# Alternating PSUM bank sets, pairing logit sums, and splitting the last outputs over two engines in a fused attention and gMLP kernel

## The chip, the core and the metric

The kernel runs on one core of a Trainium2 chip. The time is the device time of one execution in microseconds (us). A run gives several timed executions, and one execution is profiled. The span of a profiled execution is 1.7 to 1.8 us shorter than its device time in the runs here. An execution counts as slow when it is over 1.5% above the fastest of the same kernel, and as fast otherwise; all times compared here are of fast executions unless the text says otherwise.

Names of engines in the profile: PE is TensorE (matmuls), PEld its weight loads, DVE is VectorE, ACT is ScalarE, POOL is GpSimd, SP is SyncE, which here only issues DMAs. PSUM (`ps` in the profile) is the memory into which PE writes its sums; the kernel uses it in banks. "SPq", "ACTq" are the queues of DMA issues on those engines.

## The reference

One input `x` of 2048 tokens by 512 features goes through a layer norm, and then through two branches whose sum is added to `x`.

```python
# A: sliding, dilated local attention; 32 heads of 16, window of 8 keys, 2 apart
q, k, v = split(xn @ wqkv)                       # wqkv 512 x 1536
logits  = einsum('bhsd,bhswd->bhsw', q, kg) * scale   # kg: a token's own key and 7 earlier ones
o       = einsum('bhsw,bhswd->bhsd', softmax(logits), vg)
A       = o @ wo
# B: gMLP; w_sp mixes all 2048 tokens
z       = gelu(xn @ w_in)                        # w_in 512 x 1792
z1, z2  = z[..., :896], layernorm(z[..., 896:])
g       = w_sp @ z2 + b_sp                       # w_sp 2048 x 2048
B       = (z1 * g) @ w_out
return x + A + B
```

## The kernel before

The kernel describes its work as tasks with the data that they read and write. A scheduler in the kernel's own Python simulates the engines from estimated durations and fixes **one order of tasks for each engine** before the program is built.

Work goes by blocks of 512 tokens (`tc` or `j`, 0 to 3). The product `w_sp @ z2` has seven columns of features. Block 0 takes all seven with plain products. Blocks 1 to 3 take three pairs of columns by seven smaller products each (a Winograd-like scheme), and the last column with plain products. A product sequence uses PSUM banks 0 and 1 and a set of two more, banks 2 and 3 or banks 4 and 5:

```python
def prod7(i, tc, gap):
    sl = n_cb[0] % 2
    n_cb[0] += 1
    X, Wb, V, Y = 0, 1, 1, 2 + 2 * sl          # Y, Z: the alternating set
    Z = Y + 1
    ...
    P(1, X, ...)                               # 8 matmuls into bank X
    gap()                                      # other matmuls are put in here
    P(5, Wb, ...)                              # needs Tn1, a weight sum made by VectorE
    cp(half(Y), half(X), ...)                  # ScalarE copies X to Y ...
    P(6, Y, ...)                               # ... before P6 adds to it
    P(2, X, ...); gap()
    P(7, Z, ...)                               # needs wB1 after VectorE's in-place sum
    P(3, Y, ...); gap()
    P(4, V, ...)                               # needs Tn4
    # VectorE: the merge (reads Y and Z), then the product with z1 ("u")
    T("dve", ... tensor_tensor(cb, PC(512 * Y, ...), wtt, ALU.add), reads=[("ps", Y), ("ps", Z), ...], name="mg")
    T("dve", ... tensor_tensor(z1T, cb, z1T, ALU.mult), name="u")
```

The plain products advance the same counter, because they share the copy buffer `cb`:

```python
def plain_slices(tc, bank_of, cuts=(4, 4, 4, 4), fc=FC - 1):
    ...                                        # 16 matmuls into one bank
    sl = n_cb[0] % 2
    n_cb[0] += 1
    cv = A("cb", 512, 1024 * sl)
    cp(cv, bank(k), ...)                       # ScalarE empties the bank
    T("dve", ... tensor_tensor(uv, cv, uv, ALU.mult), name="up")
```

The logits: VectorE multiplies queries and shifted keys for a quarter `c` of the features (a "logit product", 128 x 4096), and PE sums over the features with weights of 128 x 32, four column tiles of the array side by side:

```python
def prod_reduce(j, c):
    T("dve", ... tensor_tensor(pbv, qb, kb, ALU.mult), writes=[("pb", s_)], prio=FILL)
    def mm(t):
        for wh in range(2):
            for g in range(4):                 # four column tiles
                last = t.matmul(PC(32 * g * PR + 3072 + 512 * wh, [[1, 512]], 32), E8[c], pb[s_],
                                start=(c == 0), stop=(c == 3))
        return last
    T("pe", mm, reads=[("pb", s_), "E8"], writes=["psl"], margin=800.0)
```

The output of a 128-token tile is summed in one bank, copied out by ScalarE and stored from ScalarE's queue (`cp(A("yout", ...), po, ...)`, then `dma("act", ...)`).

Two more pieces are used by experiments: a small bias difference that VectorE makes for each of the blocks 1 to 3, and the loads of V for the attention:

```python
def bdiff(tc):
    T("dve", ... tensor_tensor(bdt[:, 0:256], bbc_right, bbc_left, ALU.subtract), reads=["bbc"], writes=["bd"])
def ld_V(j, par):                              # even and odd tokens of block j, 1.15 MB each
    return dma("sp", lambda e: e.dma_start(A("Ve", 4608, 4608 * par), src), ...)
```

## Time and profile before

The time before is 242.76 us (median of 3, 242.71 to 243.29). The profiled execution has a span of 242.4 us; its own device time was 244.2 us.

| what | value | where it is read |
|---|---|---|
| PE busy | 235.1 us, 97% of the span | busy time by engine |
| VectorE busy | 195.4 us, 81%; 31.4 of 32 us between 172 and 204 us | windows |
| PE waits after the start | 2.5 us, two waits | list of waits |
| one group of logit sums | 0.55 us, and 0.11 us more for the run after it | chain of waits |
| end without matmuls | 3.4 us | timeline |

The page of the kernel before: span and busy tenths in 40 equal slices.

```profile
span 242.4 us, 3719 instructions
...
PE   7999999999999999999999999999699999999994
...
DVE  3687879989989998999989999769999999912010
```

PE is full from the second slice to the last but one, except in slice 29, where the longer of the waits below lies. VectorE is busy for seven tenths or more in every slice from the third to the thirty-fifth, but for one with six. The windows view of the kernel before has, for each stretch, its length and then busy us and instruction counts of PE, PEld, DVE, ACT and POOL, the granted clock, the DMA share and GB/s:

```profile
25.00:94.00 69.00, 69.00 (x413) 28.34 (x412) 63.79 (x83) 54.95 (x112) 30.39 (x31) 1.00 0.57 136
...
133.00:172.00 39.00, 37.76 (x266) 26.33 (x264) 34.93 (x29) 16.59 (x38) 0.00 (x0) 1.00 0.95 229
172.00:204.00 32.00, 30.82 (x225) 22.32 (x225) 31.38 (x27) 15.18 (x36) 0.00 (x0) 1.00 0.57 153
```

Between 25 and 94 us PE has no gap at all. Between 133 and 204 us it loses 2.4 us. PE's list of waits in the kernel before (total us, times, longest) names the cause:

```profile
PE ps L1089 <- ACT ps L1016: 2.5, 2, 2.0
```

L1089 is the matmul of the seven products, L1016 is every copy by ScalarE. The timeline of the kernel before around the longer of the two waits (start, duration, instruction; in brackets the idle time of that engine just before it, and who ended it):

```profile
159.53 2.29 DVE L1138 TENSOR_TENSOR arena<-arena 128x4096 bf16<-128x4096 bf16 x1 [3.20 <-DMA arena<-vscr]
...
171.67 0.68 DVE L1113 TENSOR_TENSOR arena<-ps,wtt 128x512 bf16<-128x512 f32 x1
172.38 0.37 ACT L1016 ACTIVATE ps<-ps 128x256 f32<-128x256 f32 x1 [3.64 <-DVE arena L1113]
...
172.81 1.92 PE L1089 MATMUL ps<-arena 128*128 128x256 bf16 x16 [2.04 <-ACT ps L1016]
```

Read upwards: PE stood 2.04 us, because ScalarE's copy into the bank stood for VectorE's merge L1113, which reads that bank. This is the border between block 1 and block 2, where two product sequences in a row use banks 2 and 3.

The chain of waits of the kernel before (start, us, what) around one group of logit sums L764:

```profile
81.81 4.32 PE ps L870 x20
86.12 0.55 PE ps L764 x8
86.67 0.97 PE ps L870 x4
```

A 512-column matmul takes 0.216 us in a long run (20 of them 4.32 us). A group of 8 is two waves of four, ideally 0.43 us; it takes 0.55, and the four matmuls after it 0.97 instead of 0.86. So a group costs 0.12 us at its start and 0.11 us at its end.

The tail of the kernel before, timeline:

```profile
239.29 0.49 ACT L1016 ACTIVATE arena<-ps 128x384 bf16<-128x384 f32 x1 [0.47 <-DMA out_dram<-arena]
239.81 0.34 ACTq L1202 DMA_DIRECT2D out_dram<-arena  x1
240.20 0.28 ACT L1016 ACTIVATE arena<-ps 128x128 bf16<-128x128 f32 x1 [0.41 <-ACT arena L1016]
240.51 0.34 ACTq L1202 DMA_DIRECT2D out_dram<-arena  x1
```

The last matmul ends near 239.0 us, and then ScalarE still empties two tiles and issues two stores alone.

### The profile page before, as it was taken

The page shows a single profiled execution, that of the slowest core. Times are in us where ns is not written, and L with a number is a line of the kernel's source. Part 1 is how long each engine was busy: PE and PEld are TensorE (multiplying, and loading weights), DVE is VectorE, ACT ScalarE, POOL GpSimd, SP SyncE. Part 2 cuts the span into 40 slices and gives each one's busy share as a digit, 9 for nine tenths or more (in the row PEclk, how much of TensorE's full clock was granted, in tenths as well). Part 3 has the DMA queues.
Part 4 walks back from the last instruction along what each step waited for, and adds up shares of the span by engine and source line. Part 5 has one row for each costly group of instructions (what it writes and reads, how often), then busy time and mean ns, then how long its engine had stood idle before and what let it go on. Part 6 is the DMA issues. An engine that isn't in the chain of part 4 may idle for free.

```text
span 242.4 us, 3719 instructions
## 1 busy us (share of the span) xinstructions
PE 235.1 (97%) x1439; PEld 129.7 (54%) x1439; DVE 195.4 (81%) x228; ACT 142.7 (59%) x293; POOL 44.1 (18%) x74
## 2 busy tenths in 40 slices
PE   7999999999999999999999999999699999999994
PEld 3444443434334434444444577776477677777652
DVE  3687879989989998999989999769999999912010
ACT  2698577946989995786811255453345434554423
POOL 4556748466044022000000000000000000000000
PEclk9999999999999999999999999999999999999999
DMA  6988999802009809706800399996973813121112
GB/s 210 361 189 177 278 326 253 120 2 87 3 0 221 212 3 221 147 4 195 260 0 0 67 281 246 293 329 148 223 207 130 252 42 65 46 65 43 32 35 87
DMA packets 61697, 35.51 MB, mean 146 GB/s; under 512 B 49388, under 2 KB 60012, under 8 KB 60656
## 3 DMA queue, kind: packets, MB, share of 16 engines
q1 hardware_dynamic: 54752, 27.73, 46.1%
q10 hardware_dynamic: 6112, 5.44, 7.7%
q0 software_dynamic: 816, 2.12, 3.3%
q8 instruction: 11, 0.18, 0.3%
q14 instruction: 6, 0.05, 0.1%
HBM read 19.01 MB, written 4.21 MB: 96 GB/s over the span
## 4 chain that ended last, share of the span: by engine, by line
PE 80%; DVE 13%; DMA 3%; ACT 2%; issue 1%; ACTq 1%; SPq 0%; DVEq 0%
PE ps L1089 15%; PE ps L730 12%; PE ps L1043 11%; PE ps L870 10%; PE ps L853 10%; PE ps L1191 10%; PE ps L710 6%; DVE arena L1138 6%; PE ps L764 4%; DVE arena L1147 3%; DMA arena<-vscr 3%; PE ps L633 2%; DVE arena L950 2%; ACT arena L1016 1%; DVE arena L1113 1%
## 5 line engine op out<-in xcount | busy, mean ns | idle before, releaser
L1089 PE MATMUL ps<-arena 128*128 128x256 bf16 x504 | 59.9, 273 | 2.5 <-ACT ps L1016 2.5
L1089 PEld LDWEIGHTS ps<-arena 128*128 128x128 bf16 x504 | 49.1, 98 | 14.5 <-ACT ps L1016 3.0
L1016 ACT ACTIVATE arena<-ps 128x512 bf16<-128x512 f32 (+3 forms) x45 | 22.6, 501 | 45.2 <-PE ps L1089 16.6
L1191 PE MATMUL ps<-arena 128*128 128x512 bf16 (+2 forms) x187 | 41.9, 366 | 0.0
L1138 DVE TENSOR_TENSOR arena<-arena 128x4096 bf16<-128x4096 bf16 x16 | 36.6, 2288 | 3.7 <-DMA arena<-vscr 3.2
L756 DVE TENSOR_TENSOR arena<-arena 128x4096 bf16<-128x4096 bf16 x16 | 36.1, 2283 | 0.0
L1043 PE MATMUL ps<-arena 128*128 128x512 bf16 x160 | 35.7, 379 | 0.0
L1147 DVE TENSOR_TENSOR arena<-arena 128x4096 bf16<-128x4096 bf16 (+2 forms) x24 | 33.6, 1400 | 0.6
L730 PE MATMUL ps<-arena 128*128 128x512 bf16 x128 | 29.3, 379 | 0.0
L1191 PEld LDWEIGHTS ps<-arena 128*128 128x128 bf16 x187 | 19.5, 108 | 13.9 <-ACT ps L1016 0.2
L853 PE MATMUL ps<-arena 128*128 128x448 bf16 x128 | 26.5, 354 | 0.1
L1043 PEld LDWEIGHTS ps<-arena 128*128 128x128 bf16 x160 | 15.7, 98 | 18.0
L870 PE MATMUL ps<-arena 128*128 128x512 bf16 x112 | 25.0, 379 | 0.0
L1016 ACT ACTIVATE ps<-arena 128x512 f32<-128x512 bf16 (+3 forms) x36 | 19.0, 534 | 7.4 <-ACT arena L1016 3.4
L738 ACT ACTIVATE arena<-ps 128x1024 bf16<-128x1024 f32 x16 | 16.3, 1021 | 7.9 <-PE ps L730 6.3
L730 PEld LDWEIGHTS ps<-arena 128*128 128x128 bf16 x128 | 12.0, 98 | 16.1 <-issue 1.7
L858 ACT ACTIVATE arena<-ps 128x448 bf16<-128x448 f32 x32 | 17.2, 546 | 4.9 <-PE ps L853 3.6
L853 PEld LDWEIGHTS ps<-arena 128*128 128x128 bf16 x128 | 11.9, 98 | 13.7 <-issue 2.3
L1016 ACT ACTIVATE ps<-ps 128x256 f32<-128x256 f32 x27 | 9.9, 367 | 15.6 <-PE ps L1089 11.3
L875 ACT ACTIVATE arena<-ps 128x512 bf16<-128x512 f32 x28 | 15.8, 601 | 5.1 <-PE ps L870 4.9
L1113 DVE TENSOR_TENSOR arena<-ps,wtt 128x512 bf16<-128x512 f32 x9 | 6.2, 685 | 15.5 <-ACT arena L1016 15.5
L870 PEld LDWEIGHTS ps<-arena 128*128 128x128 bf16 x112 | 10.6, 98 | 13.9 <-issue 0.8
(66 smaller groups left out, 230.9 us busy)
## 6 DMA issues: line engine op xcount, KB each, us to landing
arena<-vscr SPq DMA_DIRECT2D x8, 1152.0 KB, 6.5
arena<-in_A_x_dram ACTq DMA_DIRECT2D x18, 128.0 KB, 2.8
vscr<-arena POOLq DMA_DIRECT2D x16, 128.0 KB, 4.9
out_dram<-arena ACTq DMA_DIRECT2D x15, 128.0 KB, 2.5
arena<-in_A_x_dram SPq DMA_DIRECT2D x14, 128.0 KB, 6.6
arena<-in_A_wqkv_dram SPq DMA_DIRECT2D x2, 512.0 KB, 7.8
arena<-in_B_w_in_dram SPq DMA_DIRECT2D x1, 896.0 KB, 6.2
arena<-in_B_w_out_dram SPq DMA_DIRECT2D x1, 896.0 KB, 5.0
```

Of the source, the lines that this page charges most:

```text
L730: last = t.matmul(bank(k + which), AC(off["wqk"] + 1024 * dc + col0, [[1, 128]]), AC(off["xnT"] + dc * S + 512 * j, [[1, 512]]), start=(dc ...
L738: T("act", lambda a: a.activation(AC(qo, [[ko - qo, 2], [1, 512]]), ps[:, 512 * k: 512 * k + 1024].rearrange("p (t n) -> p t n", t=2), ACT ...
L756: T("dve", lambda v: v.tensor_tensor(pbv, qb, kb, ALU.mult), reads=rd, writes=[("pb", s_)], est=c_dve(4096, 2.0), name="prod%d_%d" % (j, c ...
L853: last = t.matmul(ps[:, 512 * k: 512 * k + HF], AC(off["xnT"] + dc * S + 128 * b, [[1, 128]]), AC(off["w_in2"] + FH * dc + c0, [[1, HF]]), ...
L858: T("act", (lambda k, hf: lambda a: a.activation(A("z2", HF, FH * b + HF * hf), ps[:, 512 * k: 512 * k + HF], ACTF.Gelu_apprx_tanh, accum_ ...
L870: lastm = t.matmul(bank(k), AC(off["w_in1"] + FH * dc + 128 * fc, [[1, 128]]), AC(off["xnT"] + dc * S + 512 * j, [[1, 512]]), start=(dc == ...
L1016: T("act", lambda a: a.activation(out_, in_, ACTF.Copy), reads=reads, writes=writes, est=c_act(n), name=name)
L1043: last = t.matmul(bank(k), AC(off["z2"] + FH * sh + 128 * fc, [[1, 128]]), AC(WT[r_] + sh * 512, [[1, 512]]), start=False, stop=(sh == NB ...
L1089: last = t.matmul(half(bk), lh(k), rh(k), start=False, stop=(k == NK - 1), skip_group_check=True)
L1138: T("dve", (lambda tv, iv, av: lambda v: v.tensor_tensor(tv, iv, av, ALU.mult))(tv, iv, av), reads=[("attn", j)] + ([("Ve", par)] if q < 2 ...
L1147: T("dve", (lambda o_, n: lambda v: v.tensor_tensor(o_, two(0, n), two(n, n), ALU.add))(o_, n), reads=[] if n > 512 else ["Vs", ("Ve", par ...
L1191: last = t.matmul(po, lh, rh, start=False, stop=(q == len(order) - 1), skip_group_check=True)
```

## The change

The intent: (1) the plain products no longer advance the counter, so that the product sequences strictly alternate their bank sets, also from one block to the next; (2) the logit sums of two quarters form one group, 8 groups of 16 matmuls instead of 16 of 8; (3) the last four outputs are emptied by ScalarE and VectorE in turn and stored from ScalarE's and SyncE's queues, out of a buffer with a place for each.

```diff
@@ plain_slices
                 sl = n_cb[0] % 2
-                n_cb[0] += 1
                 cv = A("cb", 512, 1024 * sl)
@@ prod_reduce
+                if c % 2 == 0:
+                    return
                 def mm(t):
                     last = None
-                    for wh in range(2):
-                        for g in range(4):
-                            last = t.matmul(... E8 + 32 * c ..., pb + 4096 * s_ ..., start=(c == 0), stop=(c == 3))
+                    for cc in (c - 1, c):
+                        sc = (s_ - c + cc) % NPB
+                        for wh in range(2):
+                            for g in range(4):
+                                last = t.matmul(... E8 + 32 * cc ..., pb + 4096 * sc ..., start=(cc == 0), stop=(cc == 3))
                     return last
-                T("pe", mm, reads=[("pb", s_), "E8"], ...
+                T("pe", mm, reads=[("pb", (s_ - 1) % NPB), ("pb", s_), "E8"], ...
@@ out_slices
+                if ends:
+                    yv, yk, en, dq = AC(off["Vs"] + 512 * (tb % 4) + c0, [[1, n]]), [("yl", tb % 4, p_)], *ends[p_]
+                else: ...                      # as before: "yout", "act", "act"
+                if en == "act":
+                    cp(yv, po, ...)
+                else:
+                    T("dve", lambda v: v.tensor_copy(yv, po), ...)
+                dma(dq, ...)
@@ the last four tiles
-                         cuts=(9, 2), banks=bk) for q, bk in zip(qord, ((6,), (7,), (yo,), (yo + 1, 6)))]
+                         cuts=(9, 2), banks=bk, ends=en)
+              for q, bk, en in zip(qord, ((6,), (7,), (yo,), (yo + 1, 6)),
+                                   ((("act", "act"),), (("dve", "sp"),), (("act", "act"),),
+                                    (("dve", "sp"), ("act", "act"))))]
```

## The prediction

> **What bounds it now.** TensorE. The table of busy time by stretches gives PE 69.00 of 69.0 us from 25 to 94 us, all of 94 to 133, and 24.94 of 25 from 204 to 229. PE's list of waits has 2.5 us at L1089, two waits for ACT. VectorE is almost as full from 33 to 212 us (31.4 of 32 between 172 and 204): the second bound. In the last 3.5 us ScalarE alone empties and stores outputs.
>
> **What each part does.**
>
> 1. *Bank sets.* Before, plain slices also advance the counter, so the last product of a 512-token block and the first of the next both use banks 2 and 3. In the timeline PE stops 2.04 us at 170.8 and 0.44 us at 203.6, because the copy into that bank (ACT L1016) waited for the VectorE merge L1113, stuck in a full queue until 171.67. Alternation removes both (2.5 us). But PE then reaches the seventh product earlier, which needs the weight sums of L950, finished at 174.2 and 205.4 us. VectorE itself moves perhaps 1.3 us (it idles 1.5 us between 94 and 133), so I estimate new PE waits of 0.1 and 0.8 us. Net 1.6 us. The plain slices of the first block now share one copy buffer; they come every 3.45 us and VectorE multiplies within about 1 us, so I expect nothing from it.
>
> 2. *Logit sums.* 16 groups of 8 matmuls (128x32 weights) become 8 of 16. Between 81.8 and 93.8 us the chain has 44 matmuls L870 and four groups; at 0.216 us per 512-column matmul (112 took 24.19) and two waves of four column tiles a group, that is 9.5 + 1.7 of 12.0 us, leaving 0.2 us a group for getting in and out. The Trainium skill, "TensorEngine Tiling (Array Packing)", Tiling Modes, says that changing the tiling mode drains TensorE; the trace agrees: weight loads pause about 0.4 us before and after a group. Eight fewer: 1.6 us, on a full PE.
>
> 3. *Tail.* PE ends near 238.9; ScalarE still has two emptyings and stores, about 1.0 us each with issue and semaphore; last store issued at 240.51. With VectorE (idle after 231.5) and a second queue taking half, the last copy follows the last matmul: store at about 239.2, 1.3 us earlier. The skill ("Trainium Kernel Development and Optimization", Key Constraints) says that issuing from several engines saves only issue time; that is what is short here.
>
> **Sum.** 1.6 + 1.6 + 1.3 = 4.5 us: **238.2 us**, 8 in 10 between **236.6 and 240.3**. 2% faster means under 237.9, near a coin toss: faster 0.40, within 2% 0.57, slower 0.03.
>
> **What would show it.** (1) PE's waits for ACT L1016 at L1089 gone; what replaces them is VectorE, L950 or L1113. (2) L764 in 8 groups of about 0.98 us in the chain, PE 1.6 us earlier by 94 us with the same 128 matmuls. (3) Last store issued 0.3 to 0.4 us after the last matmul, DVE copies beside ACT's, SP issuing two stores.
>
> **What would make it wrong.** VectorE is so full that PE's earlier arrival is eaten at the two borders (then 239.5 to 240). A scheduler fixes the order from estimates: changed dependences may reorder VectorE and move waits by 1 us either way. The single copy buffer may block ScalarE in the first block. SP's store may land later. If a logit group's in-and-out cost is not per group, part 2 gives nothing.

## The result, and the profile after

The changed kernel took 240.55 us (median of 4, 240.1 to 240.87) against 242.74 us (242.6 to 243.29) for the kernel before. The ratio is 0.9904, with a 95% interval of 0.9881 to 0.9927. Here and below a ratio is the mean time of one kernel's fast runs over that of the other's of the same rounds, so it is not quite the ratio of the medians. The change gains 2.2 us where 4.5 were foretold; 240.55 lies just above the range, and 2% was not reached.

The page of the changed kernel:

```profile
span 238.6 us, 3721 instructions
...
PE   7799999999999999999999999999999999999996
...
DVE  4588679989998998999998999989999999952022
```

The span fell by 3.8 us, but the time by only 2.2: the first trace of the kernel before was of a slower execution. PE's list of waits in the changed kernel:

```profile
PE ps L636 <- DVE fpool L545: 1.3, 1, 1.3
PE ps L861 <- DMA arena<-in_B_w_in_dram: 1.2, 1, 1.2
PE ps L772 <- DVE arena L759: 0.5, 1, 0.5
...
PE ps L878 <- ACT arena L883: 0.2, 1, 0.2
```

L636 and L861 lie in the first 9 us. The waits for ScalarE at the shared banks are gone, and nothing replaced them in the product stage, as the timeline of the changed kernel at the same border shows (L1120 is the merge, L1096 the products):

```profile
157.90 2.29 DVE L1145 TENSOR_TENSOR arena<-arena 128x4096 bf16<-128x4096 bf16 x1 [0.86 <-DMA arena<-vscr]
...
169.87 2.78 PE L1096 MATMUL ps<-arena 128*128 128x256 bf16 x24
170.10 0.68 DVE L1120 TENSOR_TENSOR arena<-ps,wtt 128x512 bf16<-128x512 f32 x1
```

PE's group of 24 started at 169.87 us, before the merge at 170.10, which it no longer needs. VectorE waited only 0.86 us for the V load this time.

The chain of waits of the changed kernel shows one pair of logit sums, L772:

```profile
38.43 3.89 PE ps L861 x20
42.32 0.98 PE ps L772 x16
43.30 0.86 PE ps L861 x4
```

16 matmuls take 0.98 us, 0.12 more than four waves of 0.216, and the four 448-column matmuls after them 0.86 us instead of 0.76. So the price of getting in and out is per group, as predicted: eight groups fewer should save 8 times 0.22, or 1.8 us.

The tail of the changed kernel:

```profile
234.22 2.42 SPq L1217 DMA_DIRECT2D out_dram<-arena  x2
...
235.72 0.56 DVE L1215 CAST arena<-ps 128x384 bf16<-128x384 f32 x1 [1.53 <-PE ps L1198]
236.33 0.28 ACT L1024 ACTIVATE arena<-ps 128x128 bf16<-128x128 f32 x1 [0.94 <-PE ps L1198]
236.64 0.34 ACTq L1217 DMA_DIRECT2D out_dram<-arena  x1
```

VectorE's copy of 384 columns took 0.56 us, and the last store is issued 0.3 us after the last matmul's end instead of 1.5.

To compare traces without the noise of the start, I cut every profiled execution at the same places of the program, read from PE's timeline: the first matmul of Q and K; the first plain product (L1043 before); the first of the seven products (L1089 before); the last run of output matmuls, whose length does not vary (9.7 us); the last matmul's end; the span's end. Stages in us:

| kernel | start | Q/K to plain | plain | products | tail | span |
|---|---|---|---|---|---|---|
| before, first trace | 14.23 | 94.19 | 27.63 | 93.25 | 3.41 | 242.4 |
| before, second trace (e1) | 13.95 | 93.99 | 27.62 | 92.10 | 3.44 | 240.8 |
| alternation only (e2) | 15.02 | 93.99 | 27.62 | 91.41 | 3.40 | 241.2 |
| pairing only (e3) | 14.03 | 93.25 | 27.62 | 92.08 | 3.42 | 240.1 |
| tail only (e4) | 14.57 | 94.40 | 27.63 | 92.14 | 2.37 | 240.8 |
| after, first trace | 14.87 | 93.70 | 27.62 | 90.42 | 2.30 | 238.6 |
| after, second trace (e5) | 14.00 | 92.75 | 27.63 | 91.06 | 2.36 | 237.5 |

Between the ordinary execution of the kernel before (e1) and the first trace after, the products give 1.7 us, the tail 1.1, the stage with the logit sums 0.3, and the start takes back 0.9: together 2.2 us. Two questions follow. Why was the wait at the banks 2.5 us in one trace, and 1.3 in others? And where did the pairing's 1.8 us go?

### The profile page after: what moved, and what is told of

It is laid out like the page before. It is cut to its first block, busy times and chain, and to the rows that moved or that the text cites. A ratio compares the mean times of both kernels' runs of the same rounds, so it can differ in the third digit from the quotient of the medians.

```text
span 238.6 us, 3721 instructions
## 1 busy us (share of the span) xinstructions
PE 232.5 (97%) x1439; PEld 131.0 (55%) x1439; DVE 196.7 (82%) x230; ACT 142.2 (60%) x291; POOL 42.3 (18%) x74
## 4 chain that ended last, share of the span: by engine, by line
PE 74%; DMA 7%; issue 6%; DVE 4%; ACT 3%; POOL 1%; SPq 1%; POOLq 1%; ACTq 1%; DVEq 0%
PE ps L1096 23%; PE ps L1198 16%; PE ps L1051 14%; PE ps L861 7%; PE ps L733 5%; DMA arena<-in_B_w_in_dram 5%; PE ps L878 4%; PE ps L772 3%; DMA arena<-in_B_b_sp_dram 2%; DVE arena L759 2%; PE ps L713 1%; POOLq L399 1%; POOL vscr L720 1%; SPq L675 1%; ACT arena L741 1%
## 5 line engine op out<-in xcount | busy, mean ns | idle before, releaser
L1096 PE MATMUL ps<-arena 128*128 128x256 bf16 x504 | 59.6, 273 | 0.0
L1096 PEld LDWEIGHTS ps<-arena 128*128 128x128 bf16 x504 | 49.3, 98 | 11.5
L1024 ACT ACTIVATE arena<-ps 128x512 bf16<-128x512 f32 (+2 forms) x43 | 21.5, 499 | 45.6 <-PE ps L1051 19.5
L759 DVE TENSOR_TENSOR arena<-arena 128x4096 bf16<-128x4096 bf16 x16 | 36.2, 2284 | 0.0
L861 PE MATMUL ps<-arena 128*128 128x448 bf16 x128 | 25.9, 353 | 1.5 <-DMA arena<-in_B_w_in_dram 1.2
L1024 ACT ACTIVATE ps<-arena 128x512 f32<-128x512 bf16 (+3 forms) x36 | 18.8, 534 | 6.4 <-ACT arena L1024 3.4
L861 PEld LDWEIGHTS ps<-arena 128*128 128x128 bf16 x128 | 12.0, 98 | 14.1 <-DMA arena<-in_B_w_in_dram 1.3
L1120 DVE TENSOR_TENSOR arena<-ps,wtt 128x512 bf16<-128x512 f32 x9 | 6.2, 685 | 14.2 <-ACT arena L1024 14.2
L1024 ACT ACTIVATE ps<-ps 128x256 f32<-128x256 f32 x27 | 9.8, 365 | 10.1 <-PE ps L1096 9.4
```

The source lines that it names most:

```text
L759: T("dve", lambda v: v.tensor_tensor(pbv, qb, kb, ALU.mult), reads=rd, writes=[("pb", s_)], est=c_dve(4096, 2.0), name="prod%d_%d" % (j, c ...
L861: last = t.matmul(ps[:, 512 * k: 512 * k + HF], AC(off["xnT"] + dc * S + 128 * b, [[1, 128]]), AC(off["w_in2"] + FH * dc + c0, [[1, HF]]), ...
L1024: T("act", lambda a: a.activation(out_, in_, ACTF.Copy), reads=reads, writes=writes, est=c_act(n), name=name)
L1096: last = t.matmul(half(bk), lh(k), rh(k), start=False, stop=(k == NK - 1), skip_group_check=True)
```

## The experiments

### One part at a time, and the kernel before again

For e1 nothing was edited. e2 has only the edit in `plain_slices`, e3 only that in `prod_reduce`, e4 only those in `out_slices` and the last tiles. A comparison of the fixed orders shows that e2 moves two ScalarE copies and nothing else, and that e4 changes only the tail, while **e3 also reorders VectorE's work** in many places.

> The kernel before, unchanged: a null control and a second trace. Theory A (the first trace of before fell in an untypical execution, since its device time was 244.2 us against 242.7 in the timed runs): the span here is near 241 us and the two waits of PE for ACT L1016 sum to 1 us or less instead of 2.5. Theory B (that trace was typical where it matters): the waits are again 2 us or more, and the extra 1.5 us of that execution lay elsewhere. The ratio is 1.000 within 0.2% under both.

> Only the strict alternation of bank sets. Prediction as recorded: 2.5 us of waits go, 1.6 us of it stays, so 241.1 us. Theory A: only what the ordinary execution waits is gained, at most 1 us (241.8 to 242.7). Theory B: 240.3 to 241.2, since the trace after the change shows no new wait for L950.

> Only the pairing of the logit sums. Prediction as recorded: 1.6 us faster (241.1). Rival: a group saved gives 0.2 us as read, but a paired group is placed behind its second product and PE stops there, and VectorE's order changes; the gain is under 0.8 us (242.0 or more), and the trace shows PE or its weight loads waiting for DVE L756 before L764.

> Only the tail with two engines and two queues: 1.3 us faster (241.4) by the prediction; the rest of the order of work is unchanged, so every other interval should be as before. Rival: the store from the second queue lands late and the gain is under 0.7 us.

| run | median us | ratio to before | 95% interval |
|---|---|---|---|
| e1, kernel before again | 242.97 | 0.9998 | 0.9975 to 1.0020 |
| e2, alternation only | 242.53 | 0.9959 | 0.9929 to 0.9990 |
| e3, pairing only | 242.37 | 0.9966 | 0.9941 to 0.9991 |
| e4, tail only | 242.47 | 0.9984 | 0.9949 to 1.0019 |

Executions of one kernel differ by 1 us and more here, so times alone hardly separate these parts. The stages of the table above do it better, though each is one execution: with one and the same order of work, the stage of the logit sums took 93.99 to 94.40 us (before, e1, e2, e4; e4's PE waited 0.34 us for a logit product), and the products 92.10 to 93.25 (before, e1, e4). The tail's gain is 1.07 us (3.44 to 2.37), not 1.3. Pairing takes 0.74 us from its stage (93.99 to 93.25), not 1.6, and, as e3's rival said, PE then waits 0.46 us for a logit product (L756). For the alternation, e1 is the key: in the second trace of the same program VectorE waited less for the V load, and PE waited less. First VectorE's timeline, then both engines' timeline, of e1:

```profile
157.73 2.29 DVE L1138 TENSOR_TENSOR arena<-arena 128x4096 bf16<-128x4096 bf16 x1 [1.89 <-DMA arena<-vscr]
```

```profile
169.94 0.68 DVE L1113 TENSOR_TENSOR arena<-ps,wtt 128x512 bf16<-128x512 f32 x1
...
171.15 1.59 PE L1089 MATMUL ps<-arena 128*128 128x256 bf16 x13 [0.87 <-ACT ps L1016]
```

The wait is 0.87 us here (and 0.47 at the second border); in e3 and e4, which share the banks too, the two sum to 1.32 and 1.38 us. The first trace's 2.48 us is the largest of all traces here. A stop of PE also costs a little more than the wait that is listed: the stage exceeds the 90.41 us that it takes without any stop (e8, below) by 1.69 us in e1 and 2.84 in the first trace, 0.17 to 0.18 us a stop beyond the waits. Theory A is right in its claim about the trace and too low by a little in its number. In e2, where VectorE waited 3.3 us for the load, the waits at the banks are gone, but PE's list of waits has a new one, for L1118, the product "u" that an output matmul needs:

```profile
PE ps L1190 <- DVE arena L1118: 0.8, 1, 0.8
```

So the alternation gives PE more room behind VectorE, not endless room. The first trace (3.20 us of waiting for the V load) and e2 (3.33) are the two to compare, because the load was about equally late in both: there the alternation takes the products from 93.25 to 91.41 us, a gain of 1.84.

### Is the late V load what makes PE wait at the banks?

The V load of block 2 is issued from SyncE's queue, which issues one load that transposes weights for 12 us just before it, as SyncE's timeline of the kernel before shows:

```profile
138.48 12.41 SPq L934 DMA_TRANSPOSE arena<-in_B_w_sp_dram  x1
...
152.29 0.58 SPq L1125 DMA_DIRECT2D arena<-vscr  x1
```

e8 is the kernel before, with that one load issued from the idle GpSimd queue; all other orders of work stay as they were. A first build of it was refused before it could run, because one semaphore served a load of each queue; e8 gives the moved load its own, and takes it out of the fixed sequence of SyncE (that line of the edit is left out here).

```diff
-            return dma("sp", lambda e: e.dma_start(A("Ve", ...), src), 128 * 4608 * 2, ("Ve", par), ...
+            return dma("pool" if (j, par) == (2, 0) else "sp", lambda e: e.dma_start(A("Ve", ...), src),
+                       128 * 4608 * 2, "VeP" if (j, par) == (2, 0) else ("Ve", par), ...
```

> The kernel before, with one load of V (third block, even tokens) issued from the idle GpSimd queue instead of SyncE's, where it stands behind the long transposing load of weights; every other order of work is the same. Theory: the wait of PE at the shared banks is set by when this load lands (first trace: VectorE waited 3.2 us for it and PE 2.04; other traces 1.3 to 1.9 and 0.75 to 0.91). Then VectorE's wait for that load goes below 0.5 us and PE's wait at the first border to about 0, while the second border keeps its 0.45; gain 0.5 to 1.0 us. Rival: PE's wait is set by VectorE's total work and stays at 0.8 us or more.

It took 241.41 us, ratio 0.9902 (0.9875 to 0.9928). The timeline of e8:

```profile
137.19 11.69 SPq L934 DMA_TRANSPOSE arena<-in_B_w_sp_dram  x1
...
145.70 0.60 POOL L1125 DMA_DIRECT2D arena<-vscr  x1 [54.19 <-DVE arena L1147]
...
167.96 0.68 DVE L1113 TENSOR_TENSOR arena<-ps,wtt 128x512 bf16<-128x512 f32 x1
...
169.03 1.15 PE L1089 MATMUL ps<-arena 128*128 128x256 bf16 x9
```

The load is issued at 145.70 us instead of 152.29 (150.40 in e1), while SyncE's queue still issues the transposing load. The merge runs at 167.96 us, before PE needs the bank, and the product stage takes 90.41 us with no PE wait at all, although the banks are still shared. The gain (2.2 us between the medians of this kernel and the kernel before of the same rounds, 1.7 in the stage) is above what I expected, because the second border's wait went too. The other traces with shared banks and the same VectorE order agree: the later VectorE got its V load, the longer PE stood at the first border (VectorE's wait and PE's: 3.20 and 2.04 us in the first trace, 1.89 and 0.87 in e1, 1.86 and 0.91 in e4, none and none in e8). So the alternation and the earlier load are two cures for the same fault, a VectorE made late by one load. e9 joins both.

> The changed kernel plus the one V load from GpSimd's queue (as in e8). The stage of products took 90.41 us without any PE wait in e8 and in the first trace after the change; e5 to e7 took 91.06 to 92.19 with VectorE waiting 2.2 to 2.7 us for that load. So 90.4 here, no PE wait for L1126 or L958, and 0.3 to 1.2 us faster than the changed kernel: 239.0 to 239.8. If the waits of e5 to e7 came from anything else, the stage stays at 91 or more.

e9 took 240.05 us, ratio 0.9828 (0.9789 to 0.9866), with 90.41 us for the products and no wait for L1126 or L958 there, as foretold. Its time missed the foretold 239.0 to 239.8 and is no better than the changed kernel's in e5 (below), since its first stage took 93.98 us: PE stood twice for a logit product there, 0.62 and 0.46 us. The next part explains that stage. e10 takes the alternation out of e9.

> As e9 but without the strict alternation of bank sets (paired sums, new tail, V load from GpSimd). If alternation is only a cushion against a late VectorE, the stage of products takes 90.4 to 90.6 here too and the time equals e9 within 0.3 us. If sharing banks at the borders costs by itself, PE waits for ACT L1016 are back and the stage takes 91 or more.

e10 took 240.69 us (median of six; one of them was slow, and the ratio of 0.9853 leaves it out). The first border has no wait, but PE waits 0.56 us for L1024 at the second, and the stage takes 91.15 us: neither a free pass for shared banks nor a cost at every border. Alternation stays worth 0.7 us there (91.15 against e9's 90.41).

### Where did the pairing's 1.8 us go?

Here is VectorE's timeline of the kernel before (L782 is the maximum of the third block's logits, L756 a merged row with the last logit product):

```profile
73.51 1.22 DVE L782 TENSOR_REDUCE fpool<-ps 128x128 f32<-128x1024 f32 x1
...
89.09 2.28 DVE L756 TENSOR_TENSOR arena<-arena 128x4096 bf16<-128x4096 bf16 x1
```

The same rows of the changed kernel (L790 and L759), and PE's timeline at the last pair:

```profile
82.79 1.19 DVE L790 TENSOR_REDUCE fpool<-ps 128x128 f32<-128x1024 f32 x1
...
94.88 2.29 DVE L759 TENSOR_TENSOR arena<-arena 128x4096 bf16<-128x4096 bf16 x1
```

```profile
97.22 1.05 PE L772 MATMUL ps<-arena 128*32 128x512 bf16 x16 [0.46 <-DVE arena L759]
```

The maximum moved from 73.5 to 82.8 us, and the last logit product from 89.1 to 94.9 us, behind layer norms and sums that it used to precede. PE came to the last pair and stood 0.46 us, and its weight loads 0.95 us. In the second trace after (e5) that product ran at

```profile
93.06 2.28 DVE L759 TENSOR_TENSOR arena<-arena 128x4096 bf16<-128x4096 bf16 x1
```

which is 1.82 us earlier. VectorE had started its run of work at 33 to 35 us, behind the small bias difference that waits for the bias load: at 34.70 us in the first trace, and at 32.90 in e5 (VectorE's timelines, the first trace after and then e5):

```profile
34.70 0.43 DVE L962 TENSOR_TENSOR bdt<-arena 128x256 f32<-128x256 bf16 x1 [1.23 <-DMA arena<-in_B_b_sp_dram]
```

```profile
32.90 0.43 DVE L962 TENSOR_TENSOR bdt<-arena 128x256 f32<-128x256 bf16 x1 [1.00 <-DMA arena<-in_B_b_sp_dram]
```

The 60.2 us between that start and the product are the same in both, so VectorE had no slack, and PE's wait depended on when the bias arrived. All five traces with this order of VectorE's work say the same:

| trace | bias difference starts after the first Q/K matmul | Q/K to plain | difference |
|---|---|---|---|
| e5 | 18.90 | 92.75 | 73.85 |
| e3 | 19.38 | 93.25 | 73.87 |
| e10 | 19.74 | 93.59 | 73.85 |
| after, first trace | 19.83 | 93.70 | 73.87 |
| e9 | 20.12 | 93.98 | 73.86 |

In this order the stage ends a fixed 73.9 us after VectorE has got the bias, so VectorE and not PE sets its length, although PE is busy nearly all of the time. Also, at 86.7 us of the first trace after, PE stood 0.18 us, and its weight loads 0.67 us, for ScalarE, which had been busy with four long squares (about 1.1 us each); in the kernel before two small logit groups fell into that time. That they covered the wait is how I read the two timelines; no run tests it alone.

> The changed kernel again, as a second trace and a better time beside before on one chip. Sum of the parts read from the traces so far: products 92.1 to 90.4 us without waits (1.4 to 1.7), tail 3.44 to 2.35 (1.1), stage from the first Q matmul to the plain slices 94.0 to 93.3-93.7 (0.3 to 0.7): 2.8 to 3.5 us in all, so 239.6 to 240.2. Rival: the times of the single parts (1.0, 0.8, 0.4) add up as timed, 2.2 us, so 240.8, and the start (first Q matmul at 14.9 instead of 14.2 us) is later for a reason and not by chance.

e5 took 240.09 us, ratio 0.9853 (0.9824 to 0.9882), a larger gain than the recorded 0.9904. Its span is 3.3 us under that of e1. So the change is worth 2.2 to 3.5 us, and the recorded run lies at the low end.

Two edits ask whether the fourth block's groups or their placing cause the loss: e6 leaves the fourth block unpaired, e7 places every pair about one group of matmuls later.

```diff
# e6
-                if c % 2 == 0:
+                if c % 2 == 0 and j < 3:
-                    for cc in (c - 1, c):
+                    for cc in ((c - 1, c) if j < 3 else (c,)):
# e7
-                  ... margin=cfg.get("m_red", 800.0))
+                  ... margin=cfg.get("m_red", 1800.0))
```

> The changed kernel, but the logit groups of the fourth token block are not paired: 10 groups instead of 8. If what pairing should save (0.22 us a group) is given back only in the fourth block, where PE waits for a second product and for ScalarE's emptying, the stage from the first Q matmul to the plain slices takes 94.0 - 6*0.22 = 92.7 us, 0.5 to 1.0 less than the changed kernel's 93.7. If the loss is not there, it takes 94.1 or more.

> The changed kernel with every logit pair placed about one group of matmuls later (scheduler margin 1.8 instead of 0.8 us), so that PE does not meet the second product. If PE's wait for the product is the loss, the stage to the plain slices takes 92.3 to 93.0 us and no wait of L772 for DVE L759 is left. If ScalarE's emptying is the loss, 93.4 or more.

e6 took 242.11 us (ratio 0.9933) and its stage 93.71 us, where I had expected 92.7. The expectation failed for a plain reason: the scheduler kept the last product behind the sums (it ran at 93.85 us) although its group was no longer paired, and PE's list of waits in e6 has

```profile
PE ps L772 <- DVE arena L759: 1.0, 1, 1.0
```

So it is the place of the product in VectorE's order that costs, not the pairing of that block. (The edit also shortens the group's list of reads to match; that line is left out above.) e7 took 240.48 us (ratio 0.9858), with 92.63 us in the stage and no wait for the product, which fits. It does not beat e5's 240.09; its products took 91.83 us, as PE waited 0.93 us for "u" after VectorE had waited 2.7 us for the V load.

The cleaner test moves the bias difference away from the head of VectorE's run, by one more dependence on a value that is made at about 91 us:

```diff
 def bdiff(tc):
-              reads=["bbc"], writes=["bd"], ...
+              reads=["bbc", ("rstd2", 3)], writes=["bd"], ...
```

> The changed kernel, with VectorE's small bias difference moved from the head of its long chain (where it stalls 1.0 to 1.9 us for the bias load, at 33 us) to behind 91 us. The two traces of the changed kernel have the last logit product 60.2 us after that stall, to 0.02 us, so the chain has no slack. Theory: PE meets the last product late because of that chain. Then the last product ends at least 1.5 us earlier relative to PE, PE does not wait for it, and the stage from the first Q matmul to the plain slices takes 92.2 to 92.7 us (e5: 92.75, first trace: 93.70). If ScalarE's emptying were the whole loss, 93.2 or more.

e11 took **238.72 us** (238.66 to 239.84), ratio 0.9783 (0.9742 to 0.9823). The timeline of e11, with the row that holds the last logit product, and the last pair:

```profile
87.61 2.29 DVE L759 TENSOR_TENSOR arena<-arena 128x4096 bf16<-128x4096 bf16 x1
...
91.25 1.05 PE L772 MATMUL ps<-arena 128*32 128x512 bf16 x16
```

The stage takes 92.23 us: 94.0 less 8 times 0.22 is 92.2. The whole saving of the pairing is there as soon as PE does not wait for VectorE or for ScalarE in this stage. One caution: the edit did two things. It removed the stall for the bias (0.6 to 1.9 us in the traces of the kernels that have it), and the scheduler, with other estimates, put the last product in front of the sums again, which is the larger move (87.6 against 93.1 us in e5). No run separates the two. The table above gives an estimate: without its stall for the bias (1.00 to 1.67 us), each of the five stages would take 91.8 to 92.5 us, as long as nothing else held PE up. So the stall alone may account for most of the loss.

### The last checks

> The kernel before with only the bias difference moved. Theory: PE never waited for a logit product in the kernel before, so the stage from the first Q matmul to the plain slices stays at 94.0 (93.8 to 94.3), and only the waits at the shared banks may shrink (stage of products 90.6 to 92.0 instead of 92.1). Rival: the move itself is what e11 gained, then the stage falls to 93 or less here too.

> e11 without the strict alternation. In e10 VectorE was early at the first border but PE still waited 0.56 us at the second, so I expect the stage of products at 91.0 to 92.0 here against 90.4 in e11, with PE waiting for ACT L1016 at one or both borders; 0.6 to 1.5 us slower than e11. If it is 90.5 or less, alternation is worth nothing once VectorE is earlier.

> e11 again, to see whether it beats both kernels on another run of the series: 238.3 to 239.3 us, ratio to before 0.976 to 0.985, stages 92.2, 27.6, 90.4 to 91.0, tail 2.35.

| run | median us | ratio to before | Q/K to plain | products |
|---|---|---|---|---|
| e13, before with the bias difference moved | 243.25 | 0.9974 (0.9935 to 1.0013) | 94.20 | 92.73 |
| e14, e11 without alternation | 240.59 | 0.9861 (0.9827 to 0.9896) | 92.44 | 92.78 |
| e15, e11 again | 239.24 | 0.9812 (0.9776 to 0.9847) | 92.44 | 91.07 |

e13 settles that the move alone gains nothing in the first stage; it only lets the pairing pay. (It missed in the products: their waits did not shrink but were 2.0 us in that trace.) e14 against e15 is the best measure of the alternation once PE is early, for VectorE waited equally long for the V load in both traces (2.03 and 2.04 us): 92.78 against 91.07 us, or 1.7 us in the stage (more than foretold) and 1.35 us between the medians. PE's list of waits in e14 shows the old wait in full:

```profile
PE ps L1097 <- ACT ps L1024: 2.0, 2, 1.6
```

e11 and e15 ran on two different chips, and both are under the changed kernel's 240.09 and 240.55, and lower in ratio (0.9783 and 0.9812 against 0.9853 and 0.9904). This version beats the kernel before by about 1.9% to 2.2%. It was never timed in the same rounds as the changed kernel; by the ratios it is faster by 0.4% to 1.2%, and the intervals of e15 and e5 overlap.

### A version that failed

e12 put everything together: alternation, pairing one group later, the tail, the bias difference moved, and the V load from GpSimd's queue.

> The changed kernel with all three: V load from GpSimd, bias difference moved, logit pairs one group later. Stages 92.5 + 27.6 + 90.4 + 9.7 + 2.35 and a start of 14.2 make a span of 236.8, a time of 238.5 us, 1.5 to 2 us under the changed kernel and faster than before by 1.8 to 2.0%. If the stages do not add up, the reordered VectorE work makes new PE waits at the two borders.

It took 253.21 us (median of six, 248.86 to 256.51). Four of the six count as slow, the profiled one among them, and the ratio of 1.0261 is that of the other two; but all six lie above every run of every other kernel here. PE's list of waits in e12, and the windows view (columns as before) before and in the middle of the wait:

```profile
PE ps L1051 <- DMA arena<-in_B_w_sp_dram: 14.2, 1, 14.2
```

```profile
157.00:160.00 3.00, 1.18 (x7) 0.45 (x5) 0.08 (x1) 0.65 (x2) 0.00 (x0) 1.00 1.08 84
...
165.00:170.00 5.00, 0.00 (x0) 0.00 (x0) 0.00 (x0) 1.20 (x2) 0.00 (x0) 0.50 1.21 63
```

The transposing load of the weights for block 2 was issued at 139.72 us and landed only at about 172 us; the DMA engines were full (share 1.21, as this view counts) but moved 63 GB/s, and with PE idle its granted clock fell to 0.50. The Trainium skill, "TensorE: Matmul & The Clock Gate", Part 1, says that an idle PE array gets half the clock after an idle window of about 3.4 us. The trace agrees on the half; the clock fell at 160.5 us, 2.3 us after the last matmul's end at 158.2, sooner than the page's figure. So in this trace the low clock followed the wait and did not start it. I asked whether the second queue's load beside the transposing loads did this by itself, with e11 plus that load, which is e12 without the later placing of the pairs:

> e11 plus the V load from GpSimd's queue. If that load colliding with the transposing loads made e12 slow, PE waits several us for the weight load here too and the time is over 245 us; if e12's later logit pairs or its other order did it, 238.3 to 239 us.

It did not: e16 took 238.94 us (two runs, 238.43 and 239.45), ratio 0.9796, with 90.41 us for the products. e8 and e9 had the same load and no collapse either, and e7 had the later placing and none. So neither edit does it alone; what their combination changes in the timing of the loads stays open.

## Why the prediction was wrong

The mechanisms of all three parts were seen at work; the sum was twice too large for the recorded runs.

1. **The step that failed most is "Eight fewer: 1.6 us, on a full PE."** The price of a group was right (0.22 us, read as 0.2). The word "full" was wrong as a proof that the saving lies on the critical path: PE was full, but VectorE was only just ahead of it. The changed dependences made the scheduler place the last logit product behind other VectorE work; from then on VectorE's chain, which starts when the bias arrives, set the length of the stage, and PE waited for the product (0.46 us), and for ScalarE (0.18 us). The stage shrank by 0.3 us in the recorded trace, by 0.7 in e3 and 1.2 in e5. With VectorE's order mended, it shrank by 1.8 us in e11 and by 1.55 in e14, e15 and e16. Of the 2.3 us missing between 4.5 and 2.2 (counted from e1's trace to the first trace after), this step has 1.3; the start of the execution (point 4) has 0.9, the tail 0.2, and the alternation gave 0.1 more than foretold.
2. **The alternation's "2.5 us" came from an execution with a late V load.** Other traces with shared banks and that load on SyncE's queue wait 1.3 to 1.4 us (e1, e3, e4) or 2.0 (e13, e14). Its net of 1.6 us was near: 1.84 us from the first trace before to e2 and 1.7 from e14 to e15, the pairs with equally late loads. That is partly luck: 0.8 of the 0.9 us taken off did come in e2, but as a wait for "u". From e1 to the recorded trace after it is 1.7 us too, but there the load was 1.0 us less late (VectorE waited 0.86 us instead of 1.89); from e1 to e5 (2.19) it is 1.0. The foretold new waits for L950 (L958 after) did not come in the first trace after; in other runs they did (1.24 us in e6, 0.19 in e15), and so did waits for "u" (0.18 to 0.93 us in e2, e5, e6 and e7), which I had not named. That the single copy buffer costs nothing was right: the plain stage takes 27.6 us in every trace.
3. **The tail's 1.3 us was mis-sized**; it measured 1.07 to 1.14 us. The last store's issue followed the matmul as foretold.
4. **The base.** The stages gain 3.1 us between e1 and the first trace after, and the recorded times 2.2. The rest is the start: the first Q/K matmul came at 13.75 to 15.02 us in the six traces without the new tail (mean 14.13) and at 14.00 to 15.21 in the twelve with it (mean 14.53). All engines have the same order of work up to that matmul before and after the change, and the four latest starts (e2, the first trace after, e12, e16; 14.87 to 15.21 us) are those in which PE waited longest for the load of `w_in` (1.0 to 1.4 us; 0.8 or less in the others). So the landing of that load makes most of the difference; whether the change has a part in it, no run was made to tell.
5. Of what the prediction named as its risks, "changed dependences may reorder VectorE and move waits by 1 us either way" is what happened. It was written down as a risk and not put into the number.

## What to carry to other kernels

A saving on a full engine is worth its size only if the engine that feeds it is early enough; before counting it, find for each input when its producer finished, and ask whether the change also moves that producer in a static order. A wait that is read from one profile should be seen in a second one: here VectorE waited 1.3 us longer for one load in one execution, and PE's wait that came of it was 2.04 us instead of 0.87. Giving a consumer another buffer and making the late producer earlier can be two cures of the same fault (e2 and e8), so their gains need not add.

## What the Trainium skill lacked or had wrong

- "TensorEngine Tiling (Array Packing)", Tiling Modes, Key Properties: it says that changing the mode drains TensorE but gives no price. Here, between 128x128 and 128x32 weights with 448 or 512 columns, a group costs 0.12 us at its start and 0.10 to 0.11 us at its end, the same for 8 and for 16 matmuls.
- "DMA: Bandwidth & Descriptors", Issuing engines are not separate DMA queues: it says that issuing from several engines only saves the issue time, which is usually small beside the transfer. Here it was not small: SyncE's queue issued one transposing load for 11.2 to 13.0 us over the 18 traces, and the V load behind it was issued at 152.29 and 150.40 us (before, e1) instead of 145.70 (e8); moving it to an idle queue gained 2.2 us.
- "Perfetto Trace Analysis" (Identifying Performance Opportunities) has nothing on how far one profiled execution may be from the next: the same wait was 2.04 and 0.87 us in two traces of one program, and the start of the first Q/K matmul varied from 13.75 to 15.21 us over the 18 traces of all kernels here.
